# State-product stores on ScalarE's queue instead of SyncE's, in a fused attention and softplus MLP kernel

## The chip, the cores and the metric

The kernel runs on one core of one Trainium2 chip. The metric is the device time of one execution in microseconds, the median of several runs. The core has TensorE (PE), VectorE (DVE), ScalarE (ACT), GpSimd (POOL) and SyncE (SP); each works through its own queue in order and waits for the others by semaphores.

## The reference

```python
# x: (8, 8, 512, 64), state: (8, 8, 32, 64), w_in: (512, 2048), w_out: (2048, 512), all float32
def _attn_ref(x, state):
    scores = scale * np.matmul(x, state.transpose(0, 1, 3, 2))        # per batch and head
    a = softmax(scores)                                               # over the 32 states
    xread = np.matmul(a, state)
    scores2 = scale * np.matmul(state, x.transpose(0, 1, 3, 2))
    a2 = softmax(scores2)                                             # over the 512 rows
    sread = np.matmul(a2, x)
    return np.concatenate([xread, sread], axis=2)                     # 544 rows per batch

def _moe_ref(x, w_in, w_out):
    h = x @ w_in
    g = np.maximum(h, 0.0) + np.log1p(np.exp(-np.abs(h)))             # softplus
    return g @ w_out
```

The two are chained: the heads of the attention output lie side by side and form 4352 rows of 512, which go through the MLP.

## The kernel before, in words

**Algebra.** For the 512 `xread` rows of a batch the kernel does not form `xread`: since `xread @ w_in = a @ (state @ w_in)`, it makes state products V = state x w_in once, and the first matrix product of the MLP (`gemm1`, L513) multiplies the attention weights `aT` with V. Softplus and the second product (`gemm2`, L520, with `w_out`) follow. Products in reduced form are made of a high and a low part of each operand (three matmuls for one); `split` (L101) makes the parts: the high one by ScalarE (L105) or GpSimd (L98), the low one by L106.

**State products of batches 0 to 3.** `make_v0` makes them for the first of four column blocks of `w_in` in eight pieces of 256 columns, `make_vf` for the three others in four pieces each. A piece is a weight tile `k` loaded by `load_w` (L112) and converted to float32 by `as_f32` on ScalarE and VectorE (L129 or L136, L131, L140, L141, L142), stored once for later (`wsc`), and multiplied by two blocks of states: `QZ[0]` for batches 0 and 1, whose product stays on the chip (`vf`), and `QZ[1]` for batches 2 and 3, whose product goes out of PSUM into a `ve` tile (two buffers) and from there to device memory (`vd`), to be fetched (L302) when batches 2 and 3 come up. The copy into `ve` is made by VectorE where the table `MOVED` names the piece, else by ScalarE (L199, L243). That is eight stores in `make_v0` (L200) and twelve in `make_vf` (L244); ten of the twenty copies are ScalarE's. All twenty stores are issued by SP.

**Order.** The strings `START`, `BLOCK` and so on give the order in which the pieces of work are written. A scheduler in the framework then sets each engine's order from the dependences and its own costs, so a change at one place moves instructions elsewhere. Weight tiles `k` have four buffers, x tiles two, the `aux` banks of PSUM two. Every DMA takes one of eight completion semaphores in turn and waits for the transfer that had it before. A DMA is issued by the queue it stands in, in order, after the waits of that DMA: what stands behind it waits too.

**Names used below.** `xT_315`, `xT_317`: x transposed for batch 1. `k_85`, `k_97`, `k_129`, `k_163`: w_out tiles; `k_100`, `k_124`, `k_137`, `k_161`, `k_185`: w_in tiles; `k_188` is ScalarE's half-way product of converting `k_185`. `wout_84`, `wout_110`, `wout_128`, `wout_162`: the first four split w_out tiles. `ghi_346`, `ghi_417`: high parts of the first two softplus tiles. `z_1259`, `xT_1264`, `xT_1266`: inputs for batch 2.

Of the kernel before, what the change touches and what calls it, by code (L numbers as in the profile page):

```python
# [49 lines left out]
def attention_then_softplus_mlp(ctx: ExitStack, tc, xn, xt, zq, zp, stk, w_in, w_out, out):  # L50
    nc = tc.nc
# [8 lines left out]
    def sb(tag, shape, dt=F32, bufs=1):  # L60
        uid[0] += 1
        return sp.tile(shape, dt, tag=tag, name=f"{tag}_{uid[0]}", bufs=bufs)
# [9 lines left out]
    def aux():  # L72
        if early[0]:
            tag = next(turn)
            return bank(tag, BANKS[tag])
        return bank("aux", 2)
# [5 lines left out]
    if WARM:  # L82
        idle = sb("sr", [P, P], bufs=2)
        nc.vector.memset(idle, 0.0)
        pb = aux()
# [34 lines left out]
    def as_f32(t, *what, tag="wt"):  # L120
        if t.dtype != I64:
            return t
        v = t.bitcast(I32).rearrange("p (n t) -> p n t", t=2)
        lo, hi = v[:, :, 0], v[:, :, 1]
        n = t.shape[1]
        h2 = sb("k2", [P, n], bufs=K2)
        r = sb(tag, [P, n], bufs=2 if tag == "wt" else 1)
        if early[0] or ("pre",) + what in MOVED:
            nc.scalar.activation(h2, f32(hi), AF.Prelu, scale=2.0 ** -112, alpha=-(2.0 ** 32))  # L129
            u = r.bitcast(I32)  # L130
            nc.vector.tensor_scalar(u, lo, 29, None, ALU.logical_shift_right)  # L131
        else:
            if ("h2",) + what in MOVED:
                nc.gpsimd.tensor_scalar(h2, f32(hi), 2.0 ** -112, 0.0, ALU.mult, ALU.add)
            else:
                nc.scalar.activation(h2, f32(hi), AF.Copy, scale=2.0 ** -112)  # L136
            u = sb("k2", [P, n], I32, bufs=K2)
            vh = t.bitcast(U16).rearrange("p (n t) -> p n t", t=4)
            uh = u.bitcast(U16).rearrange("p (n t) -> p n t", t=2)
            nc.vector.tensor_scalar(uh[:, :, 0], vh[:, :, 1], 13, None, ALU.logical_shift_right)  # L140
            nc.vector.tensor_scalar(uh[:, :, 1], vh[:, :, 3], 0x8000, None, ALU.bitwise_and)  # L141
        nc.vector.scalar_tensor_tensor(r.bitcast(I32), h2.bitcast(I32), 3, u, ALU.logical_shift_left, ALU.bitwise_or)  # L142
        return r
# [21 lines left out]
    Vd = {}  # L165
# [6 lines left out]
    Vf, Vhl = {}, {}  # L172
    made = {}

    def make_v0():
        for b in range(2):
            Vf[b, 0] = sb("vf", [P, 2, 512], bufs=2)
        for half in range(2):
            cs = slice(256 * half, 256 * half + 256)
            for q in range(4):  # L180
                k = 4 * half + q
                wt = as_f32(first.pop(0), 0, half, q, tag=f"wout{4 + k}" if k < 6 else "wt")
                nc.sync.dma_start(wsc[0][P * q:P * q + P, cs], wt)
                pb = aux()
                nc.tensor.matmul(pb[:, 0:256], QZ[0][:, q, :], wt, start=True, stop=True)
                r = slice(64 * (q % 2), 64 * (q % 2) + 64)
                for b in range(2):
                    dst, src = Vf[b, 0][r, q // 2, cs], pb[64 * b:64 * b + 64, 0:256]
                    if ("v0", half, q, b) in MOVED:
                        nc.vector.tensor_copy(dst, src)  # L190
                    else:
                        nc.scalar.copy(dst, src)
                pb = aux()
                nc.tensor.matmul(pb[:, 0:256], QZ[1][:, q, :], wt, start=True, stop=True)
                ve = sb("ve", [P, 256], bufs=2)
                if ("v0", half, q, 2) in MOVED:
                    nc.vector.tensor_copy(ve, pb[:, 0:256])
                else:
                    nc.scalar.copy(ve, pb[:, 0:256])  # L199
                nc.sync.dma_start(Vd[0, 0][:, q, cs], ve)  # L200
                made["v0", half] = q
                yield

# [9 lines left out]
    def ahead(k):  # L213
        if not come[k]:
            load_ahead(k)
        return come[k].pop(0)

    def make_vf(cs):
        for c in cs:
            for b in range(2):  # L220
                Vf[b, c] = sb(VTAGS[c][b], [P, 2, 512], bufs=2 if c == 3 else 1)
            for q in range(4):
                wf = as_f32(ahead("in"), c, q, tag="wout12" if (4 * c + q) % 3 == 2 else "wt")
                nc.sync.dma_start(wsc[c][P * q:P * q + P, :], wf)
                yield
                pb = aux()
                nc.tensor.matmul(pb, QZ[0][:, q, :], wf, start=True, stop=True)  # L227
                r = slice(64 * (q % 2), 64 * (q % 2) + 64)
                for b in range(2):
                    dst, src = Vf[b, c][r, q // 2], pb[64 * b:64 * b + 64]  # L230
                    if ("vd", c, q, b) in MOVED:
                        nc.vector.tensor_copy(dst, src)
                    else:
                        nc.scalar.copy(dst, src)
                made["v", c] = q
                yield
                pb = aux()
                nc.tensor.matmul(pb, QZ[1][:, q, :], wf, start=True, stop=True)  # L238
                ve = sb("ve", [P, 512], bufs=2)
                if ("ve", 0, c, 2 * q + 1) in MOVED:  # L240
                    nc.vector.tensor_copy(ve, pb)
                else:
                    nc.scalar.copy(ve, pb)  # L243
                nc.sync.dma_start(Vd[0, c][:, q, :], ve)  # L244
                made[0, c] = q
                yield

# [390 lines left out]
    def run(plan, b0=0):  # L638
        for what in plan:
# [24 lines left out]
            elif what in "Fp":  # L664
                work = fetches if what == "F" else pieces
                if work:
                    f, args = work.pop(0)
                    f(*args)

    v0 = make_v0()  # L670
    v_first = make_vf(range(1, 4))
    v_second = chain(prep_stk, lambda: make_v(range(4), 2))
    att[0] = attention(0, ATT[0])
# [56 lines left out]
def build(ins):  # L730
    import concourse.bacc as _bacc

    nc = _bacc.Bacc("TRN2", target_bir_lowering=False, num_devices=1)
    args = []
    for name, (shape, dt) in ins.items():
        args.append(nc.dram_tensor(f"in_{name}_dram", shape, dt, kind="ExternalInput").ap())
    for i, (shape, dtype) in enumerate(_OUTS):
        args.append(nc.dram_tensor(f"out_{i}_dram", shape, F32, kind="ExternalOutput").ap())
    with tile.TileContext(nc) as tc:
        attention_then_softplus_mlp(tc, *args)  # L740
    return nc
# [10 lines left out]
```

## Time and profile before

| | us |
|---|---|
| median of 3 runs | 697.38 (695.21 to 698.46) |
| the profiled execution | 697.26 |
| its span in the profile | 695.4 |
| TensorE busy in the span | 675.9 (97%) |
| VectorE, ScalarE, GpSimd busy | 395.0, 390.9, 218.4 |

In rows of the profile a line such as L520 is the line of the kernel above; SPq is SP's queue, where each row is the issue of a transfer, not its run. `out<-in` names the tiles, `[2.76 <-POOL wout L98]` behind a row is the idle time of the engine just before it and what ended it. A stage is a stretch of the span in us. The row of a stage gives busy time of PE, PE's weight loads, DVE, ACT and POOL, then the granted TensorE clock (1.00 is full), the busy share of the 16 transfer engines and their GB/s. "us to landing" runs from a transfer's issue to its last byte.

### The profile page before, as it was taken

Reading aid. Unit: us, or ns where it says so; the run is one execution under the profiler, and the core shown is the slowest. Engines: PE = TensorE matmul, PEld = TensorE weight load, DVE = VectorE, ACT = ScalarE, POOL = GpSimd, SP = SyncE. Lnnn points to the kernel's source line nnn. Section 1 sums busy time; section 2 is a strip of 40 time slices with the busy share of each in tenths; the row PEclk is TensorE's granted clock in tenths of the full one; section 3 lists DMA queues with packets and bytes.
Section 4 is the critical chain, followed back from the end, with each engine's and each line's share of the span. In section 5 each row is a group of like instructions: output and inputs, shape, how many; then the busy total and the mean of one; then the engine's idle time right before and its main releaser. Section 6 shows DMA issues by size and latency. Waiting matters only on the chain.

```text
span 695.4 us, 8922 instructions
## 1 busy us (share of the span) xinstructions
PE 675.9 (97%) x3028; PEld 540.1 (78%) x3028; DVE 395.0 (57%) x692; ACT 390.9 (56%) x661; POOL 218.4 (31%) x209
## 2 busy tenths in 40 slices
PE   7879999999999999999999999999999999999997
PEld 4456667788887877888888888888888889988886
DVE  5898788319777885776556752676257423311101
ACT  4787975434848944775538634863386334423321
POOL 0130157146433584156222450235022400121310
PEclk9999999999999999999999999999999999999999
DMA  7778895103253545464423220321121113512001
GB/s 253 258 258 293 307 301 188 49 0 122 68 167 122 184 156 166 143 199 136 134 94 121 69 90 31 107 76 31 31 69 45 40 39 98 168 30 61 1 0 61
DMA packets 42061, 82.90 MB, mean 119 GB/s; under 512 B 6176, under 2 KB 13088, under 8 KB 42016
## 3 DMA queue, kind: packets, MB, share of 16 engines
q1 hardware_dynamic: 42016, 82.33, 36.1%
q8 instruction: 24, 0.39, 0.2%
q14 instruction: 21, 0.17, 0.1%
HBM read 56.62 MB, written 25.69 MB: 118 GB/s over the span
## 4 chain that ended last, share of the span: by engine, by line
PE 83%; ACT 7%; DVE 5%; DMA 2%; issue 1%; POOL 1%; SPq 0%; POOLq 0%; DVEq 0%; ACTq 0%
PE acc L520 49%; PE h L513 22%; PE h L560 3%; PE aux L262 2%; PE aux L449 2%; PE aux L375 1%; ACT L500 1%; DMA xT<-in_xt_dram 1%; ACT t L500 1%; PE aux L425 1%; PE aux L238 1%; PE aux L227 1%; DMA k<-in_w_in_dram 1%; ACT ghi L105 1%; DVE glo L106 1%
## 5 line engine op out<-in xcount | busy, mean ns | idle before, releaser
L520 PE MATMUL acc<-wout,ghi 128*128 128x512 f32 x1088 | 341.7, 395 | 3.9 <-POOL wout L98 2.8
L520 PEld LDWEIGHTS acc<-wout,ghi 128*128 128x128 f32 x1088 | 203.8, 189 | 50.7 <-issue 3.6
L520 PE MATMUL acc<-wout,glo 128*128 128x512 f32 x544 | 214.2, 394 | 0.0
L513 PE MATMUL h<-aT,vhl 128*128 128x512 f32 x768 | 199.4, 398 | 0.1
L513 PEld LDWEIGHTS h<-aT,vhl 128*128 128x128 f32 x768 | 142.1, 188 | 35.3 <-issue 3.4
L500 ACT ACTIVATE t<-h 128x512 f32<-128x512 f32 x136 | 81.0, 598 | 121.4 <-PE h L513 81.1
L106 DVE TENSOR_TENSOR glo<-t,ghi 128x512 fp32r<-128x512 f32 x83 | 63.7, 770 | 124.2 <-ACT ghi L105 83.9
L106 POOL TENSOR_TENSOR glo<-t,ghi 128x512 fp32r<-128x512 f32 x53 | 70.9, 1338 | 159.5 <-ACT ghi L105 156.7
L520 PEld LDWEIGHTS acc<-wout,glo 128*128 128x128 f32 x544 | 102.4, 188 | 23.0 <-issue 0.7
L105 ACT CAST ghi<-t 128x512 fp32r<-128x512 f32 x96 | 59.1, 618 | 76.1 <-PE acc L520 75.6
L106 DVE TENSOR_TENSOR vhl<-vf,vhl 128x512 fp32r<-128x512 f32 x57 | 41.5, 728 | 58.6 <-ACT vhl L105 48.4
L98 POOL TENSOR_SCALAR ghi<-t 128x512 fp32r<-128x512 f32 x40 | 28.7, 718 | 82.1 <-PE acc L520 39.5
L105 ACT CAST vhl<-vf 128x512 fp32r<-128x512 f32 x60 | 37.1, 618 | 17.3 <-PE h L513 11.3
L500 ACT ACT_TABLE_LOAD x23 | 29.5, 1283 | 7.8 <-DVE glo L106 5.7
L380 DVE TENSOR_TENSOR sc<-aux,k 64x512 f32<-64x512 f32 x24 | 16.4, 683 | 23.4 <-ACT k L379 23.1
L98 POOL TENSOR_SCALAR vhl<-vf 128x512 fp32r<-128x512 f32 x12 | 8.4, 696 | 66.8 <-PE h L513 50.7
L277 DVE TENSOR_TENSOR R<-wt,R 64x512 fp32r<-64x512 f32 x23 | 18.8, 819 | 10.4 <-ACT R L276 7.3
L560 PEld LDWEIGHTS h<-sreadT,vhl 128*128 128x128 f32 x192 | 24.1, 191 | 0.6
L560 PE MATMUL h<-sreadT,vhl 128*128 128x256 f32 x192 | 24.3, 283 | 0.0
L106 POOL TENSOR_TENSOR vhl<-vf,vhl 128x512 fp32r<-128x512 f32 x15 | 21.9, 1457 | 6.4 <-ACT vhl L105 6.0
L262 PE MATMUL aux<-R,StK 128*128 128x512 f32 x64 | 19.1, 398 | 1.2 <-POOL R L277 0.7
L398 POOL TENSOR_TENSOR T<-T,mx 128x512 f32<-128x512 f32 x7 | 7.7, 1106 | 37.3 <-DVE mx L397 17.4
(156 smaller groups left out, 736.3 us busy)
## 6 DMA issues: line engine op xcount, KB each, us to landing
vd<-ve SPq DMA_DIRECT2D x44, 256.0 KB, 2.7
xT<-in_xt_dram SPq DMA_DIRECT2D x16, 512.0 KB, 3.7
k<-in_w_out_dram SPq DMA_DIRECT2D x16, 512.0 KB, 5.1
x<-in_xn_dram SPq DMA_DIRECT2D x16, 512.0 KB, 3.5
vf<-vd SPq DMA_DIRECT2D x64, 128.0 KB, 2.6
k<-in_w_in_dram SPq DMA_DIRECT2D x12, 512.0 KB, 4.9
out_dram<-o SPq DMA_DIRECT2D x24, 256.0 KB, 2.2
vf<-vd SPq DMA_DIRECT2D x16, 256.0 KB, 4.0
```

The source lines that it names most:

```text
L98: nc.gpsimd.tensor_scalar(dst, src, 1.0, 0.0, ALU.mult, ALU.add)
L105: nc.scalar.copy(hi, src)
L106: vec(*what).tensor_tensor(lo, src, f32(hi), ALU.subtract)
L262: nc.tensor.matmul(pb, StK[i][:, h, :], r, start=(i == 0), stop=(i == 1))
L277: vec("R", *what, o).tensor_tensor(r[z], wf[a], f32(r[a]), ALU.subtract)
L380: nc.vector.tensor_tensor(sc[64 * j:64 * j + 64], pb[0:64], s2, ALU.add)
L398: vec("tmul", bk, g).tensor_tensor(T, T, sm.unsqueeze(2).broadcast_to([P, 16, NS]), ALU.mult)
L449: nc.tensor.matmul(pb[:, 256 * j:256 * j + 256], a2T[:, c, j].rearrange("p i n -> p (i n)"), v["xs"][j][:, c].rearrange("p i n -> p (i n)" ...
L500: nc.scalar.activation(t, h, AF.Softplus)
L513: nc.tensor.matmul(h, Vhl[b, ft // 2][:, vi, g, cs], aT[b][:, ai, g], start=(n == 0), stop=(n == 5))
L520: nc.tensor.matmul(acc[c], g[gi][:, c0:c0 + P], wout[ft][:, wi], start=(ft == first and i == 0), stop=(ft == last and i == 2))
L560: nc.tensor.matmul(h[:, 256 * i:256 * i + 256], Whl[u, i][:, wi, kt, :], sreadT[:, si, kt, :], start=(n == 0), stop=(n == 11))
```

## The change

The copies out of PSUM stay on the engine that had them. A store whose copy ScalarE made is issued by ScalarE, right behind the copy in program order; a store whose copy VectorE made stays with SP. The later stores of batches 4 to 7 (L268) stay with SP too.

```diff
+    def copy_out(ve, pb, dst, *what):
+        if what in MOVED:
+            nc.vector.tensor_copy(ve, pb)
+            nc.sync.dma_start(dst, ve)
+        else:
+            nc.scalar.copy(ve, pb)
+            nc.scalar.dma_start(dst, ve)
...
                 ve = sb("ve", [P, 256], bufs=2)
-                if ("v0", half, q, 2) in MOVED:
-                    nc.vector.tensor_copy(ve, pb[:, 0:256])
-                else:
-                    nc.scalar.copy(ve, pb[:, 0:256])
-                nc.sync.dma_start(Vd[0, 0][:, q, cs], ve)
+                copy_out(ve, pb[:, 0:256], Vd[0, 0][:, q, cs], "v0", half, q, 2)
...
                 ve = sb("ve", [P, 512], bufs=2)
-                if ("ve", 0, c, 2 * q + 1) in MOVED:
-                    nc.vector.tensor_copy(ve, pb)
-                else:
-                    nc.scalar.copy(ve, pb)
-                nc.sync.dma_start(Vd[0, c][:, q, :], ve)
+                copy_out(ve, pb, Vd[0, c][:, q, :], "ve", 0, c, 2 * q + 1)
```

SP's queue at the first state products, before (about 17 to 28 us). `wsc` rows store converted weights, `Z_84` and `xT` rows load for batch 1:

```order
L200 DMA vd_0_90<-ve_143 128x256
L200 DMA vd_0_90<-ve_163 128x256
L183 DMA wsc_86<-wout_55_233 128x256
L183 DMA wsc_86<-wt_253 128x256
L334 DMA Z_84<-in_zp_dram 128x2x64 x2
L200 DMA vd_0_90<-ve_185 128x256
L200 DMA vd_0_90<-ve_205 128x256
L322 DMA xT_315<-in_xt_dram 128x1024
L183 DMA wsc_86<-wt_277 128x256
L200 DMA vd_0_90<-ve_224 128x256
L200 DMA vd_0_90<-ve_244 128x256
L322 DMA xT_317<-in_xt_dram 128x1024
```

The same place of SP's queue after the change:

```order
L192 DMA wsc_86<-wout_55_233 128x256
L335 DMA Z_84<-in_zp_dram 128x2x64
L192 DMA wsc_86<-wt_253 128x256
L335 DMA Z_84<-in_zp_dram 128x2x64
L323 DMA xT_315<-in_xt_dram 128x1024
L179 DMA vd_0_90<-ve_185 128x256
L192 DMA wsc_86<-wt_277 128x256
L323 DMA xT_317<-in_xt_dram 128x1024
L112 DMA k_85_328<-in_w_out_dram 128x512
L179 DMA vd_0_90<-ve_224 128x256
L179 DMA vd_0_90<-ve_244 128x256
```

The stores of `ve_143`, `ve_163` and `ve_205` are gone from SP, and those of `ve_224` and `ve_244` stand behind `xT_317` and `k_85` instead of ahead of them.

SP's queue after the change at about the second w_in block. Before, the store of `ve_438` stood ahead of `k_161`, that of `ve_471` ahead of the third `wsc` row here, the two x loads ahead of `k_185`, and `z_1259` and the two `xT` loads some twenty rows further down:

```order
L112 DMA k_161_568<-in_w_in_dram 128x512
L338 DMA z_1259<-in_zp_dram 128x256
L323 DMA xT_1264<-in_xt_dram 128x1024
L323 DMA xT_1266<-in_xt_dram 128x1024
L229 DMA wsc_87<-wout_126_444 128x512
L112 DMA k_163_571<-in_w_out_dram 128x512
L112 DMA k_176_614<-in_w_out_dram 128x512
L112 DMA k_179_621<-in_w_out_dram 128x512
L229 DMA wsc_87<-wt_477 128x512
L112 DMA k_185_649<-in_w_in_dram 128x512
L328 DMA x_532<-in_xn_dram 128x1024
L328 DMA x_560<-in_xn_dram 128x1024
```

The loads for batch 2 moved up, and `k_185` moved ahead of the x loads `x_532` and `x_560`.

ScalarE at the end of batch 0's and in batch 1's attention (about 57 to 66 us), before. `sr`, `sreadT` and `a2T` rows belong to the attention, `t` and `ghi` to softplus:

```order
L457 ACTIVATE sr_125<-aux_499,rs_248 128x2x2x64
L105 CAST sreadT<-aux_506 64x2x32
L433 COPY a2T_524<-aux_519 128x512
L500 ACTIVATE t_687<-h_680 128x512
L105 CAST sreadT<-aux_506 64x2x32
L105 CAST ghi_689<-t_687 128x512
L105 CAST sreadT<-aux_506 64x2x32
L433 COPY a2T_524<-aux_526 128x512
L500 ACTIVATE t_727<-h_720 128x512
L105 CAST sreadT<-aux_506 64x2x32
L136 ACTIVATE k_188_653<-k_185_649 128x512
L136 ACTIVATE k_195_671<-k_176_614 128x512
```

The same place of ScalarE after the change:

```order
L105 CAST zhl_1261<-z_1259 128x4x64
L458 ACTIVATE sr_125<-aux_499,rs_248 128x2x2x64
L136 ACTIVATE k_188_653<-k_185_649 128x512
L105 CAST sreadT<-aux_506 64x2x32
L136 ACTIVATE k_195_671<-k_176_614 128x512
L105 CAST sreadT<-aux_506 64x2x32
L434 COPY a2T_524<-aux_519 128x512
L501 ACTIVATE t_687<-h_680 128x512
L105 CAST sreadT<-aux_506 64x2x32
L105 CAST ghi_689<-t_687 128x512
L105 CAST sreadT<-aux_506 64x2x32
L434 COPY a2T_524<-aux_526 128x512
```

The conversion of `k_185` and that of `k_176` moved ahead of the casts and copies, and the cast of `z_1259` came in.

On TensorE the order changes only up to the first eighty rows or so; there eleven of the twelve L520 matmuls on `wout_128` stand ahead of the first product with `wt_477`, where three of them did.

## The prediction

> **What bounds the kernel now.** I read the page's slices first, then busy time by stage, then the waits and the order of time on SP's queue, and last ScalarE's and VectorE's rows at the two places where TensorE stops.
>
> ```profile
> PE   7879999999999999999999999999999999999997
> DMA  7778895103253545464423220321121113512001
> ...
> core 0: us, PE busy (x) PEld busy (x) DVE busy (x) ACT busy (x) POOL busy (x), PEclk, DMA share, GB/s
> ...
> 10.00:20.00 10.00, 7.28 (x27) 4.47 (x26) 9.73 (x30) 8.64 (x23) 1.05 (x1) 1.00 0.75 265
> 20.00:30.00 10.00, 8.42 (x33) 5.00 (x33) 9.19 (x19) 7.47 (x15) 1.67 (x2) 1.00 0.78 227
> 30.00:40.00 10.00, 5.96 (x17) 3.87 (x18) 7.37 (x20) 7.80 (x14) 0.99 (x1) 0.89 0.79 300
> 40.00:50.00 10.00, 10.00 (x35) 6.54 (x34) 9.77 (x23) 7.78 (x12) 3.78 (x3) 0.94 0.69 221
> ...
> 70.00:80.00 10.00, 9.99 (x36) 6.35 (x36) 6.62 (x15) 9.78 (x20) 1.28 (x1) 1.00 0.81 286
> 80.00:90.00 10.00, 10.00 (x42) 7.57 (x41) 8.07 (x15) 9.92 (x17) 4.49 (x3) 1.00 0.90 329
> ...
> 300.00:400.00 100.00, 99.95 (x454) 81.82 (x453) 63.89 (x111) 62.07 (x103) 41.57 (x38) 1.00 0.36 120
> ```
>
> From about 100 us on TensorE is full (99.95 of 100 us in the sample row), and behind 110 us the change leaves the order of the engines nearly as it was. So the time changes only by what TensorE's idle time before 107 us changes. There VectorE (10 to 30 and 40 to 50 us), ScalarE (70 to 90 us, 9.78 and 9.92 of 10) and the transfers (share 0.69 to 0.90) are each close to full in turn. A gain in one stage can be lost in the next.
>
> **The stores on SP's queue.** Ten of the twenty stores leave SP: those of `ve` tiles that ScalarE copied (four of 128 KB at L200, six of 256 KB at L244).
>
> ```profile
> SPq L244 <- ACT ve L243: 9.8, 5, 3.6
> SPq L200 <- ACT ve L199: 2.3, 2, 1.5
> L244 SPq DMA_DIRECT2D vd<-ve x10: 319/327/382, 45.5 to 108.2; - x10
> L200 SPq DMA_DIRECT2D vd<-ve x8: 319/326/383, 17.2 to 28.2; - x8
> ```
>
> SP stood 12.1 us (9.8 + 2.3) in front of such stores with loads behind them, and spent 10 x 0.33 = 3.3 us on issuing them. Nothing else of the two functions changes: same copies, same matmuls, same bytes.
>
> The Trainium skill, DMA: Bandwidth & Descriptors, section Issuing engines are not separate DMA queues, speaks against a gain: issuing from several engines saves only the sequencer's issue time, which is small. By it the saving would be those 3.3 us of SP time, none of it on TensorE's path, and the sum zero; the 12.1 us are what the sentence leaves out.
>
> **Step 1: the loads leave earlier.**
>
> ```profile
> 17.23 0.79 SPq L200 DMA_DIRECT2D vd<-ve  x2
> ...
> 20.79 0.80 SPq L200 DMA_DIRECT2D vd<-ve  x2
> 21.64 0.44 SPq L322 DMA_DIRECT2D xT<-in_xt_dram  x1
> ...
> 24.06 0.79 SPq L200 DMA_DIRECT2D vd<-ve  x2
> 24.91 0.42 SPq L322 DMA_DIRECT2D xT<-in_xt_dram  x1
> 25.38 0.44 SPq L112 DMA_DIRECT2D k<-in_w_out_dram  x1
> ...
> xT<-in_xt_dram SPq DMA_DIRECT2D x1, 512.0 KB, 6.3
> k<-in_w_out_dram SPq DMA_DIRECT2D x1, 512.0 KB, 7.1
> ```
>
> The first two stores and the second of the next pair go to ScalarE, and the order puts the 24.06 pair behind `xT_317` and `k_85` instead of ahead. That takes 0.79 + 0.40 + 0.79 = 2.0 us of issuing out from in front of `k_85`, and the waits of SP between 22.6 and 24.06 us. I put `xT_315` at about 19.1, `k_85` at about 21.5 us, 3.9 us earlier. It cannot land that much earlier for certain, since the transfers have room only for what their share leaves: 25% of ten us and 22% of the 4.5 us to 24.5, about 3.5 us. I take 3.3 us: `k_85` lands at 29.2 instead of 32.5 us (25.38 + 7.1). Bounds: 0 (transfers full) and 3.9.
>
> **Step 2: the first gemm2 starts earlier.**
>
> ```profile
> 32.52 0.69 ACT L129 ACTIVATE k<-k 128x512 f32<-128x512 f32 x1 [1.10 <-DMA k<-in_w_out_dram]
> ...
> 33.31 0.72 DVE L383 STREAM_TRANSPOSE T<-aux 128x512 f32<-128x512 f32 x1 [0.36 <-PE aux L369]
> 35.83 0.69 DVE L142 SCALAR_TENSOR_TENSOR wt<-k,wt 128x512 int32<-128x512 int32 x1
> ...
> 36.61 0.99 POOL L98 TENSOR_SCALAR wout<-wt 128x512 fp32r<-128x512 f32 x1 [11.28 <-DVE wt L142]
> ...
> 37.65 4.61 PE acc L520 x12
> ...
> 176.30 2.72 PE acc L520 x12
> ```
>
> Now VectorE does batch 1's softmax block (33.31 to 35.83) between the load and the combining at L142; the new order puts L142 ahead of it. From landing to first L520 was 5.1 us (32.52 to 37.65). New, on ScalarE: k 0.6, ve 0.4, a table load 1.28, t 0.6, ghi 0.6, together 3.5, and VectorE and GpSimd are ready as early. So 29.2 + 3.5 = 32.7 us, 5.0 earlier. The twelve matmuls took 4.61 us where later ones take 2.72, with the granted clock at 0.89 and 0.94 around them, after a gap that would nearly close: another 1.7. In all 6.7 us ahead at the end of this group.
>
> **Step 3: most of it is given back.** The second group needs `ghi_417`, and in the new order ScalarE does three table loads and nine operations between the two.
>
> ```profile
> 45.20 1.09 PE L520 MATMUL acc<-wout,ghi 128*128 128x512 f32 x4
> ...
> L500 ACT ACT_TABLE_LOAD x6 | 7.7, 1283 | 0.1
> L136 ACT ACTIVATE k<-k 128x512 f32<-128x512 f32 x16 | 10.6, 673 | 2.2 <-DMA k<-in_w_in_dram 2.2
> ```
>
> 3 x 1.28 + 9 x 0.63 = 9.5 us behind 32.7: 42.2 us instead of 45.20, a lead of 3.0. VectorE, full there, carries about that lead to `wout_128`, and the order then lets eight more L520 matmuls go first.
>
> **Step 4: ScalarE waits for `k_185`.** In the new order its conversion `k_188` stands ahead of the four sreadT casts and two a2T copies that free the bank for the transposes of `aux_526`; before, it stood behind them.
>
> ```profile
> 57.33 0.47 ACT L457 ACTIVATE sr<-aux,rs 128x256 f32<-128x256 f32 x1 [0.99 <-PE aux L443]
> 64.28 1.27 ACT L136 ACTIVATE k<-k 128x512 f32<-128x512 f32 x2 [2.20 <-DMA k<-in_w_in_dram]
> ...
> 55.57 2.08 SPq L327 DMA_DIRECT2D x<-in_xn_dram  x2
> 57.76 0.37 SPq L112 DMA_DIRECT2D k<-in_w_in_dram  x1
> ...
> k<-in_w_in_dram SPq DMA_DIRECT2D x1, 512.0 KB, 6.5
> k<-in_w_in_dram SPq DMA_DIRECT2D x1, 512.0 KB, 3.8
> ...
> 59.50 0.60 PE L425 MATMUL aux<-ident,sc 128*128 128x128 f32 x4
> ...
> 66.10 1.12 PE L227 MATMUL aux<-wt,QZ 128*128 128x512 f32 x2
> ```
>
> `k_185` took 6.5 us behind two x loads; `k_137` (the 3.8 row) had nothing ahead. Now `k_185` is issued ahead of the x loads, once its buffer is free, at about 53.5 us by the lead of step 3, so I take 4.0 us: landed at 57.5. ScalarE arrives at about 56 and waits 1.5. The chain behind it (two k, a2T, t, ghi, four short casts, a VectorE subtraction: 3.9 us) frees the bank at 61.4 where the transposes ran at 59.50 before. From there to L227 stands 5.9 us of matmuls: 67.3 against 66.10, 1.2 late, but with six L520 matmuls (6 x 0.227 = 1.4) done that used to come later. Lead left: 0.2. The cast of `z_1259` (0.4 of ScalarE) also moves out of the full stretch up to 90 us: 0.6 in all.
>
> **The new stores on ScalarE.** No row shows a DMA issued there. The nearest price is SP's 0.33 each; the longest SP issue of a 512 KB load, 1.38, I take as the upper end. Six of the ten have an operation between copy and store that covers the issue; the first two do not, and cost about 0.65 at 17.5 us, where the cast of `vhl_319` (0.6) moves away and pays it; the last ones fall behind 96 us, where TensorE has work in hand. Each store also waits for the transfer that had its completion semaphore before; the one to watch is `ve_471`, which waits for `k_161`, and `k_161` no longer stands behind the store of `ve_438`. I take 0 net, bounds 0 and 2 x 1.38 = 2.8. The Trainium skill, Perfetto Trace Analysis, section DMA Instruction — HWDGE (DVE, Sync), says that the descriptor generator is shared and locked, so a store on a second queue may wait for SP's issue; by it each uncovered store costs one SP issue more. No row shows it.
>
> 1.15 MB for batch 2 (`z_1259`, `xT_1264`, `xT_1266`) move from 74 us to about 43 us, ahead of `k_163`, into a stage with a transfer share of 0.69: free 3.1 us in ten, which they fill (3.8 us at 300 GB/s) without holding up `k_163`, as SP waits there for VectorE anyway. Two more table loads (2.6 us) come behind 105 us, with TensorE ahead: 0.
>
> Sum: 0.2 + 0.4 = 0.6 us saved. The profiled execution is 697.26 us (span 695.4 and 1.9 around it), 0.12 below the median 697.38. Forecast 696.7 us.
>
> **Rivals.** *Larger gain.* The loads land as much earlier as they leave (3.9 instead of 3.3), and `k_185` is there when ScalarE comes: steps 2 and 3 keep about 3 us plus 1.4 for the matmuls done early: 692.9. For it: SP's 12.1 us. Against it: a share of 0.75 to 0.79. *Slower.* `k_185` lands no earlier than before, 64.2 us, because the moved loads and the buffer it waits for hold it. Then ScalarE and, behind it, TensorE stand still from 56 to 64.2 instead of to 57.5: 6.7 us on the forecast, 703.4. Each us that it lands behind 57.5 costs one; from 61.7 on the kernel is slower by over 0.5%. For it: before, the same load ended a wait of 2.20 us. Against it: it is now ahead of the x loads. *No change:* the transfers set the stage, what leaves earlier lands no earlier, and only issue time is saved: 697.3. For it: shares of 0.75 to 0.90; against it: 12.1 us in which SP issued nothing while the share was below 1. The rule on issuing engines above would give the same time.
>
> **How the numbers follow.** About 0.5%, 3.5 us, is what a measurement can tell from no change. Chances: forecast 0.38 (own range 694.5 to 698.5), larger gain 0.28, slower 0.22, no change 0.12. The larger gain counts as faster, with 0.03 of the forecast: 0.31. The slower case counts mostly as slower, with a little of the forecast: 0.22. The rest, 0.47, is within. The range takes in most of the larger gain and the slower case up to some 4.3 us of added wait: 692.3 to 701.0.
>
> **What would show it.** `k_85` issued near 21.5 us; the first L520 near 32.7 us with a granted clock near 1 from 30 to 50 us; the second group near 42 us; ScalarE idle in front of L136 near 56 us, ended by a k load; L425 near 61 us. The forecast is wrong if that wait is absent or over 4 us, or if ScalarE shows long store issues with VectorE and TensorE waiting for it.

## The result, and the profile after

| | before | after |
|---|---|---|
| median, us | 697.92 (4 runs, 695.21 to 698.54) | 702.43 (4 runs, 700.95 to 703.14) |
| ratio, 95% interval | | 1.0062 (1.0039 to 1.0085) |
| profiled execution, span | 697.26, 695.4 | 702.3, 700.4 |

The kernel became slower by 4.5 us. I had forecast 0.6 us faster. First, the stores. The page's rows of the transfer queues show that they went where they should: 2.10 MB on a queue of their own, q10, ScalarE's.

```profile
q1 hardware_dynamic: 40576, 80.24, 35.6%
q10 hardware_dynamic: 1440, 2.10, 0.9%
```

Next, ScalarE's rows of the changed kernel in order of time. An ACTq row is the issue of a store.

```profile
18.16 0.84 ACTq L182 DMA_DIRECT2D vd<-ve  x2
19.04 1.13 ACT L201 COPY vf<-acc 64x256 f32<-64x256 f32 x3 [0.64 <-PE acc L203]
...
31.32 0.68 ACT L129 ACTIVATE k<-k 128x512 f32<-128x512 f32 x1 [3.06 <-DMA k<-in_w_out_dram]
...
44.94 0.67 ACT L136 ACTIVATE k<-k 128x512 f32<-128x512 f32 x1
45.08 0.33 ACTq L182 DMA_DIRECT2D vd<-ve  x1
...
60.78 0.70 ACT L136 ACTIVATE k<-k 128x512 f32<-128x512 f32 x1 [1.25 <-DMA k<-in_w_in_dram]
```

An issue costs 0.33 us, as on SP, and the one at 45.08 runs beside the conversion that started at 44.94 and ends at 45.61. Only the first pair stands in the open, and the copy behind it (19.04) waited for TensorE anyway. The last row is the wait that step 4 forecast: `k_188` waits for `k_185`, in front of the copies that TensorE needs.

SP's rows answer to step 1: `xT_315`, `k_85`, and further down `k_185` and the x loads behind it.

```profile
20.08 0.60 SPq L323 DMA_DIRECT2D xT<-in_xt_dram  x1
21.92 0.32 SPq L179 DMA_DIRECT2D vd<-ve  x1
23.18 0.32 SPq L192 DMA_DIRECT2D wsc<-wt  x1
23.55 0.43 SPq L323 DMA_DIRECT2D xT<-in_xt_dram  x1
24.07 0.38 SPq L112 DMA_DIRECT2D k<-in_w_out_dram  x1
...
54.23 0.33 SPq L229 DMA_DIRECT2D wsc<-wt  x1
56.17 0.33 SPq L112 DMA_DIRECT2D k<-in_w_in_dram  x1
57.32 2.05 SPq L328 DMA_DIRECT2D x<-in_xn_dram  x2
```

And TensorE's rows at the same points of the program as in the prediction: first gemm2, second group, the transposes of `aux_526`, the product of `aux_609`, and one more that the prediction did not have.

```profile
35.77 0.85 PE L521 MATMUL acc<-wout,ghi 128*128 128x512 f32 x3
...
44.10 1.33 PE L521 MATMUL acc<-wout,ghi 128*128 128x512 f32 x4 [0.38 <-ACT ghi L105]
...
62.75 0.66 PE L426 MATMUL aux<-ident,sc 128*128 128x128 f32 x4 [1.14 <-ACT a2T L434]
...
69.62 1.12 PE L232 MATMUL aux<-wt,QZ 128*128 128x512 f32 x2
...
100.27 1.12 PE L232 MATMUL aux<-wt,QZ 128*128 128x512 f32 x2 [2.07 <-DVE wout L237]
```

The gain is there at first: 35.77 against 37.65, 44.10 against 45.20. At 62.75 it has turned into a loss (59.50 before), though TensorE has done six more matmuls than before when it comes to the product of `aux_609` (200 records against 194). The last row is a wait of 2.07 us for a copy by VectorE.

Stages say how much of the 5.0 us between the two spans lies where. A stage's length less TensorE's busy time is TensorE's idle time there. Before, then after:

```profile
57.00:80.00 23.00, 22.40 (x89) 14.27 (x88) 17.04 (x38) 19.11 (x39) 1.28 (x1) 1.00 0.83 290
80.00:110.00 30.00, 28.88 (x113) 20.82 (x112) 23.54 (x36) 24.99 (x39) 13.70 (x11) 1.00 0.93 317
...
215.00:235.00 20.00, 19.72 (x86) 14.94 (x85) 15.44 (x29) 18.09 (x29) 4.48 (x4) 1.00 0.58 198
```

```profile
57.00:80.00 23.00, 20.77 (x84) 13.53 (x83) 18.05 (x37) 18.14 (x39) 2.00 (x2) 1.00 0.89 302
80.00:110.00 30.00, 27.93 (x107) 19.69 (x106) 23.28 (x34) 24.42 (x37) 11.42 (x9) 1.00 0.72 243
...
215.00:235.00 20.00, 18.05 (x78) 13.80 (x77) 13.64 (x27) 16.16 (x24) 4.04 (x4) 1.00 0.47 161
```

From 57 to 80 us the idle time grew by 1.63 us (0.60 to 2.23), from 80 to 110 by 0.95 (1.12 to 2.07), from 215 to 235 by 1.67 (0.28 to 1.95). That is 4.25 of the 5.0. Which of these belong to the change, and which to the one execution that was profiled, the experiments had to say.

### The profile page after: what moved, and what is told of

The parts are those of the page before. It is cut to its first block, busy times and chain, and to the rows that moved or that the text cites. A ratio compares the mean times of both kernels' runs of the same rounds, so it can differ in the third digit from the quotient of the medians.

```text
span 700.4 us, 8913 instructions
## 1 busy us (share of the span) xinstructions
PE 677.1 (97%) x3028; PEld 539.1 (77%) x3028; DVE 396.6 (57%) x692; ACT 393.5 (56%) x663; POOL 216.3 (31%) x209
## 4 chain that ended last, share of the span: by engine, by line
PE 80%; ACT 7%; DVE 5%; DMA 4%; issue 2%; POOL 2%; SPq 0%; POOLq 0%; ACTq 0%; DVEq 0%
PE acc L521 47%; PE h L514 21%; PE h L561 3%; PE aux L263 2%; PE aux L450 2%; PE aux L376 1%; DMA k<-in_w_in_dram 1%; DMA k<-in_w_out_dram 1%; ACT t L501 1%; DMA xT<-in_xt_dram 1%; ACT L501 1%; DMA out_dram<-StK 1%; DVE k L140 1%; PE aux L426 1%; DVE wt L142 1%
## 5 line engine op out<-in xcount | busy, mean ns | idle before, releaser
L514 PE MATMUL h<-aT,vhl 128*128 128x512 f32 x768 | 199.2, 397 | 1.0 <-ACT t L501 0.8
L514 PEld LDWEIGHTS h<-aT,vhl 128*128 128x128 f32 x768 | 142.1, 188 | 36.7 <-issue 3.7
L106 DVE TENSOR_TENSOR glo<-t,ghi 128x512 fp32r<-128x512 f32 x83 | 64.2, 776 | 124.8 <-ACT ghi L105 84.1
L106 POOL TENSOR_TENSOR glo<-t,ghi 128x512 fp32r<-128x512 f32 x53 | 71.3, 1345 | 154.0 <-ACT ghi L105 151.2
L106 DVE TENSOR_TENSOR vhl<-vf,vhl 128x512 fp32r<-128x512 f32 x57 | 40.3, 709 | 58.6 <-ACT vhl L105 48.5
L98 POOL TENSOR_SCALAR ghi<-t 128x512 fp32r<-128x512 f32 x40 | 26.5, 662 | 81.2 <-PE acc L521 39.5
L106 POOL TENSOR_TENSOR vhl<-vf,vhl 128x512 fp32r<-128x512 f32 x15 | 21.8, 1455 | 6.4 <-ACT vhl L105 6.0
```

The lines of the kernel that those rows point to most:

```text
L98: nc.gpsimd.tensor_scalar(dst, src, 1.0, 0.0, ALU.mult, ALU.add)
L106: vec(*what).tensor_tensor(lo, src, f32(hi), ALU.subtract)
L514: nc.tensor.matmul(h, Vhl[b, ft // 2][:, vi, g, cs], aT[b][:, ai, g], start=(n == 0), stop=(n == 5))
```

## The experiments

Both kernels write their instructions in the same sequence; only the scheduler's order per engine differs. So an order can be carried from one to the other. The experiments take the lists of either kernel and hold each engine to a list by edges within the engine, which set the order of issue and add no wait on another engine:

```diff
+    for row in ORDER.values():            # one list per engine
+        for a, b in zip(row, row[1:]):
+            tc.add_manual_dep(traced[b], traced[a].name, how, reason="hold_order")
```

Theory S: the stores on ScalarE's queue cost by themselves. Theory O: the new order costs. Later P (a place at 60 us) and Q (a place near 99 us) for where in the order, and R (ahead of 57 us). In the summary at the end of this section stands TensorE's idle time by stage for every run.

**The same kernel again (after_again).**

> The changed kernel itself, unaltered, to see what of its trace returns. If the loss is the program's own: 4 to 5 us above the kernel before (ratio 1.005 to 1.008), the first batch-0 scores' transposes of batch 1 (L426) near 62.8 us, the batch-1 product L232 (aux_609) near 69.6, and the 1.65 us wait of TensorE near 227 us for the stk copy, with a store of StK that lands after more than 5 us. If parts of it are chance of the one profiled execution, those parts are gone from this trace: without the wait at 227 us the span would be near 698.5 us, without the late start 0.5 us less again, and the ratio falls towards 1.002.

Measured: 701.68 us against 696.75, ratio 1.007 (1.0048 to 1.0093). The waits at 62 us (1.31), 99 us (2.07) and near 226 us (1.36) all came back; the loss is the program's own. The last of the three turned out not to belong to the change, as the second profile of the kernel before shows below.

**The stores alone (e1): ten stores on ScalarE, everything else in the order of before.**

```diff
 # ScalarE's list: that of before, with
  L181 COPY ve_123 <- aux_122
  L136 ACTIVATE k_125 <- k_124
+ L182 DMA vd <- ve_123              (ten such stores; SP's list loses its ten)
```

> The ten stores on ScalarE's queue, but every engine's other instructions held in the order of the kernel before (a store stands one instruction behind its copy on ScalarE, the first two directly behind). Theory O (the loss comes from the order that the scheduler made): no loss, between 696.0 and 698.5 us against 697.9 before, and a gain of up to 1.5 us if the loads behind the stores on SyncE then leave earlier. Theory S (the second queue or the issue on ScalarE costs by itself): 700.5 to 703 us, with the same waits of TensorE between 40 and 110 us as in the changed kernel.

Measured: 696.45 us against 696.75, ratio 0.9998 (0.9982 to 1.0014). Within the interval, ten stores on the second queue cost nothing and bring nothing. Theory S is out.

**The order alone (e2): all stores back on SP, everything else in the order of the changed kernel.**

> The reverse: all stores on SyncE, and every engine's other instructions held in the order of the changed kernel. Theory O: the loss stays, 700.5 to 704 us. Theory S: 697 to 698.5 us, as before.

Measured: 702.52 us, ratio 1.0081 (1.0061 to 1.0101). The whole loss is there without one store on ScalarE. These two runs decide it: the change moved the time through the scheduler's order alone.

**Batch 2's loads (e3).**

```diff
 # SP's list
   z_1259
-  xT_1264, xT_1266
   wsc <- wout12_126
...
   k_248
+  xT_1264, xT_1266
```

> The changed kernel with its own orders, but batch 2's two xT loads (1.05 MB together), which it issues at 41 us, are put back on SyncE to where the kernel before has them, behind the load of k_248 (about 75 us). If these loads take the DMA engines away from the weight loads between 40 and 50 us (share 1.00 there): k_185 lands 2 to 3 us earlier (58 instead of 60.8 us), the L426 transposes come at 60.5 to 61.5 instead of 62.75, and the time is 1.5 to 3 us below the changed kernel's (699.5 to 701). If the loss comes from the order of the casts on ScalarE and VectorE: 701.5 to 703, with the L426 transposes at 62 to 63.

Measured: 702.04 us, ratio 1.0068 (1.0049 to 1.0087), no better. The share of the transfer engines from 40 to 50 us fell from 0.91 (after_again) to 0.63, and `k_188` waited longer all the same (2.31 us). `k_185` was issued at 55.29, since SP waited in front of it for VectorE (L141), not for those loads. So batch 2's loads, and the full transfer engines from 40 to 50 us, were not the cause.

**The place at 60 us (e4), and three cuts in time (h57, g57, h80).** In e4 the conversions of `k_185` and `k_176` move behind the copies:

```diff
 # ScalarE's list (VectorE's three steps of k_185 and two of k_176 go behind the sreadT rows likewise)
-  L136 k_188 <- k_185
   L105 sreadT <- aux_506
-  L136 k_195 <- k_176
...
   L434 a2T <- aux_526
+  L136 k_188 <- k_185
+  L136 k_195 <- k_176
```

> The changed kernel with its own orders except one place: the conversion of the weights in k_185 (its first step on ScalarE, k_188, and its three on VectorE) and that of k_176 go behind the copies of batch 1's scores, as in the kernel before. Theory P (the loss starts there: ScalarE stands 1.4 us for k_185 in front of the copies that TensorE waits for at 62 us): that wait of 1.3 us is gone, 0.8 to 2 us come back (700.0 to 701.2 against 701.7 to 702.5), and if the wait of 2.1 us near 99 us only follows from it, 3 to 5 us (697 to 699). Theory Q (the loss lies in VectorE's order between 80 and 100 us) or theory R (it lies ahead of 57 us): 701.5 to 703 us.

Measured: 701.02 us, ratio 1.0054 (1.0037 to 1.0071), 1.1 us under the ratio of after_again ((1.007 - 1.0054) x 697), which the intervals do not separate. The wait at 62 us is gone, but another takes its place four microseconds on, for a copy that now stands behind the moved steps on VectorE:

```profile
66.52 1.99 PE L444 MATMUL aux<-x,a2T 128*128 128x256 f32 x8 [1.25 <-DVE ve L178]
```

The cuts hold all engines to one kernel's lists for what starts ahead of a time, and to the other's for the rest. All have the stores on ScalarE.

> Stores on ScalarE's queue; every engine follows the changed kernel's order for what starts in its first 57 us, and the order of the kernel before for all that is left. If the loss lies behind 57 us (theories P and Q): 695.5 to 698 us, like the kernel before. If what was done ahead of 57 us (batch 2's loads first, the second group's order) causes it (theory R): 701 to 703.

Measured: 698.3 us, ratio 1.0011 (0.9997 to 1.0024).

> The reverse: the order of the kernel before for what starts in its first 57 us, the changed kernel's for the rest. Theories P and Q: the loss stays, 700.5 to 703 us. Theory R: 696 to 698.

Measured: 709.74 us, ratio 1.0164 (1.0138 to 1.019), worse than either kernel. The mixture has `k_188` in front of the copies, and the load of `k_185` late (issued at 58.53). ScalarE, then TensorE:

```profile
66.83 0.69 ACT L136 ACTIVATE k<-k 128x512 f32<-128x512 f32 x1 [5.75 <-DMA k<-in_w_in_dram]
...
68.82 1.11 PE L426 MATMUL aux<-ident,sc 128*128 128x128 f32 x4 [6.11 <-ACT a2T L434]
```

> As the kernel with the cut at 57 us, with the cut at 80 us. Theory P (the place at 60 us): most of the loss stays, 699.5 to 702.5 us. Theory Q (80 to 100 us): 696 to 698.5.

Measured: 699.12 us, ratio 1.0021 (1.0009 to 1.0032). So some 1.5 us of the loss arise ahead of 80 us, and the larger part behind it. h57 lies 0.8 us above the kernel before, and its interval includes a ratio of 1; yet TensorE stood idle for 2.00 us from 57 to 80 us in it, though its order there is that of before. So what makes that idle time may be laid ahead of 57 us. g57 is like the rival "slower" of the prediction: `k_188` starts 6.05 us later than in the changed kernel (66.83 against 60.78), TensorE's idle time from 57 to 80 us is 4.7 us longer (6.89 against 2.23), and the time is 6.6 us longer ((1.0164 - 1.007) x 697). So most of what `k_185` lands too late is paid.

**A second profile of the kernel before (before_again).**

> The kernel before, unaltered, for a second profile. If its wait of 1.12 us near 97 us (a product L227 that waits for VectorE's copy L232) and its quiet place near 222 us (no wait for the stk copies) belong to the program, both return. If they are chance of the one profiled execution, the first is 0 to 2 us and the second 0 to 1.7 us this time.

Measured: 698.21 us. The wait near 97 us is gone, and there is one of 1.42 us at 222.8 us, where the first had none. TensorE's idle time from 80 to 110 us is 0, from 215 to 235 us 1.71. So the wait for the stk copies comes and goes with the execution, on both sides of the change, and must be left out of its account. The wait near 97 us also comes and goes in the kernel before; in the changed kernel's order it was 2.07 to 2.12 us in every profile that left this place as it is (after, after_again, e2, e3, e4). Its row in the first profile of the kernel before:

```profile
97.24 1.13 PE L227 MATMUL aux<-wt,QZ 128*128 128x512 f32 x2 [1.12 <-DVE wout L232]
```

**One copy of VectorE moved (e5).**

```diff
 # VectorE's list
   L142 wt_290 <- k_289
+  L237 wout14_187 <- aux_265
   L140, L141 k_302 <- k_263
   L140, L141 k_305 <- k_272
-  L237 wout14_187 <- aux_265
   L142 wout12_304 <- k_303
```

> The changed kernel with its own orders except one instruction: VectorE's copy of the second half of the third chunk's first product (L237, wout14_187 out of aux_265) goes ahead of four conversion steps (k_302 and k_305) instead of behind them. Theory Q (that copy holds up TensorE near 99 us): the wait of 2.07 us there is gone and 2 to 3.5 us come back, 698.5 to 700.3 us, about the kernel with the cut at 80 us. If the wait only moves (the next product waits for the conversions that now come later): 701 to 702.5 us.

Measured: 698.51 us, ratio 1.0022 (1.0006 to 1.0038), the same as the cut at 80 us. One instruction, 0.69 us long, moved up by four places, takes back about 3.3 us ((1.007 - 1.0022) x 697) of the loss; each of the two ratios is known to 1 to 1.6 us. A wait of 2.07 us that the rows show is gone; the rest is not placed, since the profiled execution was 0.8 us ahead already at the product of `aux_609` (68.30 against 69.08). VectorE's list in the changed kernel's second profile shows why the copy was late:

```profile
93.83 1.77 DVE L142 SCALAR_TENSOR_TENSOR wt<-k,wt 128x512 int32<-128x512 int32 x1
95.53 0.92 DVE L140 TENSOR_SCALAR k<-k 128x512 uint16<-128x512 uint16 x1
96.34 0.89 DVE L141 TENSOR_SCALAR k<-k 128x512 uint16<-128x512 uint16 x1
97.13 1.50 DVE L140 TENSOR_SCALAR k<-k 128x512 uint16<-128x512 uint16 x1
98.53 0.44 DVE L141 TENSOR_SCALAR k<-k 128x512 uint16<-128x512 uint16 x1
99.00 0.69 DVE L237 COPY wout<-aux 64x512 f32<-64x512 f32 x1
```

ScalarE copied the other half of the same bank from 95.46 to 96.04. In e5 VectorE's copy starts as ScalarE's ends; here VectorE came to it only at 99.00.

**GpSimd relieved (e7): two conversion steps of GpSimd done by ScalarE.**

```diff
-MOVED has ('h2', 3, 2), ('h2', 8)     # GpSimd takes these two steps
+MOVED without them                    # ScalarE takes them, behind the softplus of t_267
```

> The changed kernel with its own orders, but two conversion steps (the high words of k_263 and k_272, L134) are done by ScalarE instead of GpSimd, right behind the softplus of t_267, where ScalarE stood idle for 1.4 us. If VectorE's instructions between 91 and 98 us take 0.9 to 1.8 us instead of 0.45 to 0.7 because GpSimd works beside them (1.8 us of its 7 us there are taken away): VectorE's copy L237 comes 1 to 2 us earlier, the wait near 99 us shrinks to 0 to 1 us, and the time is 700 to 701.5. If the order alone sets it: the wait stays at 2 us and the time at 701.5 to 703.

Measured: 701.76 us, ratio 1.0069 (1.0047 to 1.009). VectorE's rows were hardly faster (1.78, 0.88, 1.53), since GpSimd's other work moved up and met them; and the two steps on ScalarE delayed a copy of ScalarE, for which TensorE now waited 1.42 us. Inconclusive on GpSimd.

**The other cut at 80 us (g80).**

> Stores on ScalarE's queue; every engine follows the order of the kernel before for what starts in its first 80 us, and the changed kernel's for the rest. With theory P's place taken out and theory Q's left in: 698.5 to 700.5 us, 2 to 3.5 above the kernel that keeps the order before throughout (696.5). If the place near 99 us costs only after a late start (its delay follows from what happened at 60 us): 696 to 698.

Measured: 698.08 us, ratio 1.0019 (0.9997 to 1.0041), 1.5 us above e1 ((1.0019 - 0.9998) x 697), less than the 2 to 3.5 expected; its wait there was 0.54 us in the profiled run, one of the fastest of the twelve. This suggests that the place near 99 us costs most when the engines arrive there as in the changed kernel, and that P and Q are not simply two terms that add. The interval, 0 to 2.9 us above the kernel before, is too wide to show it.

**Both places (e8): e5, and the place at 60 us repaired again.** VectorE's copy `ve_152` and ScalarE's L458 copies go ahead this time:

```diff
 # ScalarE's list behind the second a2T copy
+  k_188, k_195, t_209, L458, k_203, ghi_210, L458, wout4, k_213, wout5, L239 ...
```

> The changed kernel with its own orders, repaired at both places: VectorE's copy of aux_265 ahead of the four conversion steps (as in the run before), and the conversions of k_185 and k_176 behind the copies of batch 1's scores on ScalarE and VectorE, this time with VectorE's copy ve_152 and ScalarE's two scaled copies (L458) ahead of them, and the store of wout12_189 behind the loads of k_193 and k_212 on SyncE. If the two places are the whole loss: 696.5 to 698 us, 0.5 to 2 below the run with the one place repaired (698.5), within 0.2% of the kernel before. If the second part arises ahead of 57 us or in the loads themselves: 698 to 699.5, no better than with one place repaired.

Measured: 701.34 us, ratio 1.0055 (1.0034 to 1.0077), worse than e5 alone. Up to the product of `aux_609` (65.48) it was ahead of every run so far, then TensorE waited 3.30 us for a copy of ScalarE (L239) that stood behind a cast of `wout5`, and that cast for VectorE:

```profile
71.13 1.11 PE L478 MATMUL aux<-ident,sr 128*128 128x128 f32 x4 [3.30 <-ACT wout L239]
```

My two repairs of the place at 60 us each made a new wait. That this place accounts for the 1.5 us of h80 is therefore not shown. The idle time stands between 57 and 80 us, and h57 has it too: whether the order there makes it, or how late each engine arrives, stays open.

**The wait for the stk copies (e9): e1 with one fetch moved.** In e1 the first half of `vf_580` is issued behind the first of the four StK stores, the second half behind all four. Only the first half moves; the expectation speaks of both.

```diff
 # SP's list
   out <- StK
-  vf_580 (first half)
   out <- StK x3
+  vf_580 (first half)
   vf_580 (second half)
```

> Stores on ScalarE's queue with the order of the kernel before, and one thing else changed: the two fetches of batch 3's last products (vf_580, 0.5 MB) go behind the last store of StK on SyncE instead of between the four (near 215 us). If the last StK store lands late (3.5 to 5 us) because those fetches share the DMA engines with it: it lands in 2 to 3.5 us, the wait of TensorE near 222 us (0 to 1.4 us, by profile) is gone, and the time is 0.5 to 1.5 us below that of the same kernel without it (695 to 696 against 696.5). If the late landing has nothing to do with them: 696 to 697.5.

Measured: 695.4 us against 697.62, ratio 0.9973 (0.9959 to 0.9988): faster than both kernels. In the one profile of each, the four StK stores land in a median of 2.1 us instead of 3.5, here e1's row, then e9's:

```profile
out_dram<-StK SPq DMA_DIRECT2D x4, 256.0 KB, 3.5
```

```profile
out_dram<-StK SPq DMA_DIRECT2D x4, 256.0 KB, 2.1
```

TensorE's wait goes by the slowest of the four stores, not by the median: the slowest landed after 4.9 us in e1, 5.3 in before_again and 5.3 in the changed kernel, where TensorE waits, after 3.7 in the first profile of the kernel before, where it does not, and after 2.3 in e9.

This wait had nothing to do with the change; taking it away is worth some 1.7 us beside e1 ((0.9998 - 0.9973) x 697). In the changed kernel's order it was not tried. e9 has the change's stores and the old order; by e1 the stores are not what makes it faster.

TensorE's idle time by stage, worked out as above (us; ratio to the kernel before). The last column is the start, in us, of twelve products of `gemm1` in a row, L513 (L514 in the changed kernel):

| run | 57 to 80 | 80 to 110 | 215 to 235 | ratio | start of the twelve L513 |
|---|---|---|---|---|---|
| before, two profiles | 0.60, 0.61 | 1.12, 0 | 0.28, 1.71 | 1 | 101.80, 100.78 |
| e1, stores alone | 0.84 | 0 | 1.24 | 0.9998 | 100.56 |
| after, two profiles | 2.23, 2.43 | 2.07, 2.07 | 1.95, 1.64 | 1.0062, 1.007 | 104.83, 104.30 |
| e2, order alone | 2.06 | 2.08 | 1.75 | 1.0081 | 104.41 |
| e3, batch 2 late | 2.56 | 2.12 | 0.28 | 1.0068 | 105.31 |
| e4, casts first | 2.36 | 2.07 | 1.27 | 1.0054 | 105.83 |
| h57 | 2.00 | 0 | 1.15 | 1.0011 | 102.28 |
| g57 | 6.89 | 2.09 | 1.22 | 1.0164 | 112.82 |
| h80 | 2.05 | 0 | 1.80 | 1.0021 | 101.91 |
| g80 | 0.46 | 0.54 | 0.28 | 1.0019 | 100.99 |
| e5, one copy ahead | 2.11 | 0 | 1.57 | 1.0022 | 101.25 |
| e7, GpSimd relieved | 2.36 | 1.42 | 1.46 | 1.0069 | 104.27 |
| e8, both places | 3.35 | 0 | 1.20 | 1.0055 | 103.09 |
| e9, fetch behind | 0.61 | 0 | 0.16 | 0.9973 | 99.62 |

The first two columns sort the runs: with e1 as the base the new order adds 1.2 to 1.7 us from 57 to 80 and 2.1 from 80 to 110, 3.3 to 3.8 together, of 4.9 to 5.8 by the medians of one comparison.

These windows stand still while the work moves through them. The last column sets the runs at one point of the program, ahead of which TensorE has done as many matmuls in either order (318 or 319 records). Before, then after:

```profile
101.80 2.88 PE L513 MATMUL h<-aT,vhl 128*128 128x512 f32 x12
```

```profile
104.83 2.88 PE L514 MATMUL h<-aT,vhl 128*128 128x512 f32 x12
```

The order of before reaches this point at 100.56 to 101.80 us (before twice, e1), the changed kernel's at 104.30 to 104.83 (after twice, e2): 2.5 to 4.3 us later. What is left of the span from there, less the idle time from 215 to 235 us, is 593.3 to 593.8 us in five of these six profiles and 594.6 in e1. So the new order costs ahead of about 105 us; behind it only the wait for the stk copies comes and goes. The medians' 4.9 to 5.8 us lie higher than these profiles show, and one execution of each kernel cannot settle the rest: the profiled execution of e1 lies 1.8 us above its median, that of before_again 1.1 above the median of the kernel before.

## Why the prediction was wrong

**Right.** The stores at nothing (e1: 0.9998); batch 2's loads at nothing (e3); that a lead would be given back at the second group; and that `k_188` would stand in front of the copies and wait (1.25 us, forecast 1.5).

**Right by luck.** The first group was forecast to run without its slow matmuls, and it did: 2.9 us (35.77 to 38.67) instead of 4.61, with a granted clock of 1.00 from 30 to 50 us. But the second profile of the kernel before has the group at 3.05 us too (39.11 to 42.16). Its first five matmuls in the first profile, then in the second:

```profile
37.65 2.45 PE L520 MATMUL acc<-wout,ghi 128*128 128x512 f32 x5 [2.76 <-POOL wout L98]
```

```profile
39.11 1.45 PE L520 MATMUL acc<-wout,ghi 128*128 128x512 f32 x5 [1.62 <-POOL wout L98]
```

So the slow matmuls belonged to one execution, and the 1.7 us that step 2 counts for them were not the change's to gain. The size of the wait of `k_188` is luck as well: `k_185` came 3.3 us later than forecast and ScalarE 3.5 us later (59.53 instead of 56), so their difference came out nearly right.

**The steps that failed.** Step 1: `k_85` was to be issued at 21.5 us and left at 24.07. I had taken out the issue times and the waits of the stores that went away. But the stores that stay wait for VectorE (L179 at 21.92, `wsc` at 23.18), and these waits came forward into the place of those removed. VectorE itself made the copy of `ve_185` later, at 21.46 instead of 20.34: its new order puts a transpose (L402) first, which waited 1.24 us for GpSimd. The groups of SP's waits show what came forward; the columns behind the engine are the us waited, the count and the longest. Before, then after:

```profile
SPq L244 <- DVE ve L241: 15.2, 5, 5.0
...
SPq L200 <- DVE ve L197: 0.8, 2, 0.4
```

```profile
SPq L179 <- DVE ve L178: 20.9, 8, 3.7
```

The waits for VectorE's copies grew from 16.0 to 20.9 us over the whole run, and SP's gain at `k_85` was 1.3 us, not 3.9. With the order of before and the same ten stores gone, e1 shows it again:

```profile
SPq L179 <- DVE ve L178: 21.0, 7, 5.7
```

There `k_85` was issued at 27.91, 7.2 us behind the Z loads (20.70); in both profiles of the kernel before it was 6.3 (25.38 and 26.45, the Z loads at 19.10 and 20.17). So the 12.1 us that the prediction set against the rule on issuing engines were not there to be gained. The Trainium skill, DMA: Bandwidth & Descriptors, section Issuing engines are not separate DMA queues, says that transfers started by several engines run on the same transfer engines, and that starting them from several saves only the time of starting them; e1 agrees with it, with 0.9998.

In step 2, ScalarE's chain behind the load took the 3.5 us forecast (31.32 to 34.81), but TensorE had six L514 products in front of the group and began it at 35.77. The lead behind step 2 was then 3.6 instead of 6.7 us, behind step 3 it was 1.1 (44.10) instead of 3.0.

Step 4: the landing of `k_185` was put at 57.5 from a lead of 3.0 that was not there. It was issued at 56.17 instead of 53.5, as SP waited 1.5 us for VectorE (L141) to be done with its buffer, and ended ScalarE's wait at 60.78, 4.6 us after its issue instead of 4.0. The product of `aux_609` came at 69.62 instead of 67.3. The rival "slower" had this mechanism in part (a late `k_185` in front of the copies; not that ScalarE itself would be late), with one microsecond for each that `k_185` lands behind 57.5; by its rule 60.8 gives 700.0.

The missing term: I let the sum end at that product. Behind it I looked at ScalarE's table loads, not at VectorE's list, and the wait of 1.12 us at 97 us, in the trace of before, I took as part of both kernels. In that execution it showed how little slack VectorE has there; in the second profile of the same kernel it is 0. The changed order made it 2.07 us. Since 1.12 of it stand in the 697.26 us from which the sum starts, it adds 0.95: 701.0 against the measured 702.43. The some 1.5 us left are no more than the wait for the stk copies alone differs between the two first profiles (0.28 and 1.95 us of idle time), which is chance of the execution; nothing else is shown for them. With 0.22 for slower I had put too little on it: of two places where the new order put a wait in front of a copy that frees a PSUM bank, I saw one.

## What to carry to other kernels

A change that moves an instruction to another queue can act through the scheduler's order alone: hold the order and test the change by itself before pricing it. When a wait is removed from an in-order queue, count the waits of the instructions that stay behind it; they come forward. Follow each engine's copies that free PSUM banks down the whole stretch in which the engines are near full, since a copy placed behind four conversions cost more here than ten stores.

## What the runs showed of the hardware that I had not expected

Where instructions of VectorE and GpSimd overlap, some take two to three times as long, and which of the two engines is slowed differs between executions of one program. In the first profile of the kernel before, GpSimd's two L134 steps took 1.90 us together, VectorE's L140 and L141 beside them 0.91 each, and the L106 that followed, beside other work of GpSimd, 1.76:

```profile
89.03 1.90 POOL L134 TENSOR_SCALAR k<-k 128x512 f32<-128x512 f32 x2
```

```profile
89.54 0.91 DVE L140 TENSOR_SCALAR k<-k 128x512 uint16<-128x512 uint16 x1
90.35 0.91 DVE L141 TENSOR_SCALAR k<-k 128x512 uint16<-128x512 uint16 x1
...
92.18 1.76 DVE L106 TENSOR_TENSOR glo<-t,ghi 128x512 fp32r<-128x512 f32 x1
```

In the second:

```profile
88.90 4.98 POOL L134 TENSOR_SCALAR k<-k 128x512 f32<-128x512 f32 x2
```

```profile
89.77 0.46 DVE L140 TENSOR_SCALAR k<-k 128x512 uint16<-128x512 uint16 x1
90.13 0.45 DVE L141 TENSOR_SCALAR k<-k 128x512 uint16<-128x512 uint16 x1
90.47 0.67 DVE L142 SCALAR_TENSOR_TENSOR wt<-k,wt 128x512 int32<-128x512 int32 x1
91.06 0.68 DVE L106 TENSOR_TENSOR glo<-t,ghi 128x512 fp32r<-128x512 f32 x1
```

Here VectorE is not slowed, and GpSimd takes 4.98 us for the two steps. In the first case TensorE waited 1.12 us near 97 us, in the second not at all. The Trainium skill, SBUF — State Buffer, section SBUF: two separate sides, says that the two share a port pair which whoever starts first holds for a whole instruction, the other blocked. One row of after_again agrees: L140, at 97.13, took 1.50 us instead of 0.45 and ended just behind this instruction of GpSimd, which had started first and ran to 98.32:

```profile
96.99 1.33 POOL L106 TENSOR_TENSOR glo<-t,ghi 128x512 fp32r<-128x512 f32 x1
```

By their spans the two L134 steps do not show that rule: VectorE's L142 started at 89.17, 0.27 us behind the first L134, and was not held up (0.68 us). L237 and L232, which read PSUM, took 0.67 to 0.69 in both profiles of either kernel.

With one 256 KB fetch issued behind the first of four 256 KB stores of StK, the stores' median landing was 3.5 us (the slowest 4.9, in e1); with it behind all four, 2.1 (2.3, in e9). All are issued by one queue, and the transfer engines' share over 215 to 235 us was only 0.56 and 0.60.
